# An attention-and-MLP kernel in new instruction orders, with fewer unused matmuls, and VectorE and GpSimd kept apart

## The chip, the cores and the metric

The kernel runs on one core of a Trainium2 chip. The core has five engines that run side by side, each in the order of its own instruction stream: TensorE (PE; its weight loads are listed apart as PEld), ScalarE (ACT), VectorE (DVE), GpSimd (POOL) and SyncE (SP, which here only issues DMA transfers). They wait for one another through semaphores. The metric is the device time of one execution in microseconds (us); smaller is better. Before the change it is 211.13 us, the median of three runs (210.77 to 211.39).

## The reference: decayed linear attention, then an MLP with a snake activation

Attention comes first, for 4 batches of 8 heads, 768 positions and 64 channels, in blocks, with a state that is carried from block to block. Its output, as 3072 tokens of 512 features, goes through an MLP of width 2048.

```python
for b in range(nb):
    intra = np.einsum('bhic,bhjc->bhij', qb, kb) * Dmask[None]
    intra = np.einsum('bhij,bhjd->bhid', intra, vb)
    inter = np.einsum('bhid,bhde->bhie', qb * lam_pow[None], kv_state)
    out[:, :, sl] = intra + inter
    kv_state = lam_block[None, :, None, None] * kv_state + np.einsum('bhsd,bhse->bhde', kb_dec, vb)
...
h = x @ w_in
s = np.sin(alpha * h)
g = h + s * s / (alpha + 1e-09)
return (g @ w_out).astype(np.float32)
```

## The kernel before

**Work.** Attention is done in 24 blocks of 128 positions (6 for each batch). A block's q and k are loaded as float32, scaled by powers of lam into bf16 (`scale_block`, L462 to L495, on DVE, POOL and ACT), transposed on PE or by DMA (`piece_Q`, `piece_K`, `piece_T`), multiplied into scores (`part_S`, L612) and masked on DVE (L623). Then come the state (`part_Z`, L648 and L656, evicted by L666 and L672) and the output (`part_O`, `piece_P` and `piece_I`, evicted by L726 and L739 into `xT`, the MLP's input, transposed). Four blocks are one chunk of 512 tokens; there are six chunks.

For each chunk and each of 16 slices of the MLP's width, `unit_A` (L822; `unit_A2`, L856, does two slices for half a chunk) multiplies w_in's slice with `xT`; ACT takes the sine (L832, L866); ACT or POOL squares it (L836 and L837, L870 and L871); DVE adds h (L839, L874) and writes `gT`. Chunks 0 and 1 are multiplied by w_out in `unit_B` (L887). For chunks 2 to 5 the second product is done with seven instead of eight block products (`product`, `unit_P`, L975). These need sums of blocks of `gT` and of w_out: `token_sums` (L953) and `weight_sums` (L930), each a TENSOR_TENSOR whose operands are all bf16 in SBUF, on DVE or POOL. `finish` and `finish_half` combine the products and store the result.

**Order.** `_Plan.op` doesn't issue anything: it appends an operation to a list of 1040, with its engine or the engines it may run on, and works out from the tiles read and written which earlier operations it depends on. `_Plan.ORDER` has a table for each engine (PE, ACT, DVE, POOL, SP) with the numbers of its operations in the order in which they are issued. Where an operation may run on two engines, the table in which its number stands decides. `_settle` takes the tables as they are, and `emit` issues the instructions with the waits that the dependencies ask for. An engine does its table strictly in order: an operation that waits holds up all behind it.

**Unused matmuls.** In PE's table a pair (n, cols) stands for n matmuls of `idle` (ones) with itself, 128 x 128 by `cols` columns, into bank 0, with a result that nobody reads (`spin`, L1134). `idle` is set by a DVE memset, op 16.

**Numbers that the prediction names.** Loads on SP: 2, 3 (q, first four blocks), 4 to 7 (k), 8 to 11 (v, in two pairs), 96 and 97 (w_in's first slices), 109 (q of blocks 4 and 5). Loads on POOL: 102 to 104 (w_in) and 105 to 108 (w_out). Start: 41 to 46, 49 and 50 scale q and k; 53, 55, 57, 59 transpose q, 61, 62, 69, 70 transpose k; 47 and 48 (POOL) cast v of blocks 0 and 1 from loads 8 and 9; 51 (ACT) and 52 (POOL) cast v of blocks 2 and 3 from loads 10 and 11; 29 and 30 (POOL) clear the two `Zd` tiles; 65, 67, 73, 78 are the scores of blocks 0 to 3; 75, 82, 87 the state after blocks 0 to 2, evicted on ACT by 76 and 77, 83 and 84, 88 and 89; 81, 86, 92, 94 evict the four outputs to `xT` (95, on DVE, half of the last); 124 and 130 are the first two units of chunk 0, which need blocks 0 and 1, and 2 and 3. Later: 195 and 196 (POOL) scale the two halves of q of blocks 4 and 5, 206 and 207 transpose them; 142, 149, 153 and others are squares; 232, 233, 235 are parts of `unit_B`; 653 is DVE's addition for a slice of chunk 3, 673 the PE piece that uses its bank, 681 a unit next to it. The end: 1028 is the product that the store 1030 needs, 1037 the last product.

Of the kernel before, what the change touches and what calls it, by code (L numbers as in the profile page):

```python
# [33 lines left out]
class _Plan:  # L34
# [17 lines left out]
        ),  # L52
        "ACT": (
# [16 lines left out]
        ),  # L70
        "DVE": (
# [1174 lines left out]
```

## Time and profile before

| | |
|---|---|
| median of three runs | 211.13 us (210.77 to 211.39) |
| profiled execution, span from its first to its last instruction | 209.8 us |
| instructions in it | 4867 |
| granted TensorE clock, as the profile shows it | 1.000 |
| HBM read, written | 27.28 MB, 6.29 MB |
| costliest group: L822 on PE, x296 | 70.5 us, 379 ns each |
| L975 on PE, its three largest groups | 16.3, 16.0 and 15.8 us |
| L887 on PE, x128 | 31.4 us, 380 ns each |

The profile is of one execution, taken by the hardware profiler. Busy time is the time in which at least one instruction of an engine ran. In a timeline row stand the start, the length, the engine, the line, the operation, the tiles out<-in, the shape and the count of instructions merged; a bracket gives the engine's idle time just before and what ended it. Ends of matmuls are modelled and overlap with the next start, so that starts tell the pace. In the chain of work that ended last a row has start, length and what it was. A row of a DMA queue has packets, megabytes and the share of 16 engines' time.

### The profile page before, as it was taken

To read this page: it belongs to the slowest core of one execution; us is meant where nothing else is said; L and a number is where in the kernel's file an instruction comes from. 1 tells how busy PE (TensorE), PEld (TensorE's weight loads), DVE (VectorE), ACT (ScalarE), POOL (GpSimd) and SP (SyncE) were. 2 spreads that over 40 slices of the span, in tenths; PEclk is the share of its full clock that TensorE was granted. 3 is DMA by queue.
4 is the path that set the end of the run, shared out by engine and by line. 5 is a ranking of instruction groups with operands and counts; after the bars stand their busy time and mean duration, and the time that the engine had idled before them with its cause. 6 is when DMAs were issued, how large, how long until landed. Compare 5 with 4: busy or idle time off the path is not lost.

```text
span 209.8 us, 4867 instructions
## 1 busy us (share of the span) xinstructions
PE 203.5 (97%) x1975; PEld 134.3 (64%) x1975; DVE 160.3 (76%) x266; ACT 158.7 (76%) x294; POOL 126.9 (60%) x130
## 2 busy tenths in 40 slices
PE   7979999999999999999998999999999999999995
PEld 6847444457677776555555667766667765666894
DVE  4884557563999866868899799889698699777643
ACT  4949995968998989999997887787963889568210
POOL 7075354994469578679885392944581957378300
DMA  4999999999998999999999920190000004000514
GB/s 141 310 318 232 206 213 237 246 229 256 220 264 205 227 245 230 223 233 196 246 271 228 213 53 0 33 271 2 3 0 3 0 23 179 3 0 0 200 40 163
DMA packets 78998, 33.35 MB, mean 159 GB/s; under 512 B 55408, under 2 KB 76160, under 8 KB 78976
## 3 DMA queue, kind: packets, MB, share of 16 engines
q1 hardware_dynamic: 73744, 27.14, 56.2%
q0 software_dynamic: 3696, 3.67, 10.5%
q10 hardware_dynamic: 1536, 2.24, 3.3%
q8 instruction: 15, 0.25, 0.5%
q14 instruction: 7, 0.06, 0.1%
HBM read 27.28 MB, written 6.29 MB: 160 GB/s over the span
## 4 chain that ended last, share of the span: by engine, by line
PE 83%; DVE 6%; DMA 3%; SPq 3%; ACT 2%; issue 1%
PE bank L822 27%; PE bank L975 22%; PE bank L887 13%; PE bank L856 10%; DMA v<-in_v_dram 3%; PE bank L716 3%; SPq L315 3%; PE bank L612 3%; DVE gT L839 2%; PE bank L694 1%; DVE Sm L623 1%; PE bank L511 1%; PE bank L656 1%; DVE w L930 1%; PE bank L534 1%; PE bank L707 1%
## 5 line engine op out<-in xcount | busy, mean ns | idle before, releaser
L822 PE MATMUL bank<-xT,w 128*128 128x512 bf16 x296 | 70.5, 379 | 0.0
L839 DVE SCALAR_TENSOR_TENSOR gT<-u,rinv,bank 128x512 bf16<-128x512 bf16 x74 | 53.6, 742 | 18.2 <-ACT u L836 12.5
L832 ACT ACTIVATE t<-bank,alpha 128x512 bf16<-128x512 f32 x74 | 50.0, 684 | 21.0 <-PE bank L822 20.5
L822 PEld LDWEIGHTS bank<-xT,w 128*128 128x128 bf16 x296 | 28.3, 98 | 28.4 <-DVE gT L839 0.4
L836 ACT ACTIVATE u<-t 128x512 bf16<-128x512 bf16 x59 | 36.5, 628 | 1.3
L837 POOL TENSOR_TENSOR u<-t 128x512 bf16<-128x512 bf16 x15 | 16.0, 1066 | 34.1 <-ACT t L832 30.5
L953 POOL TENSOR_TENSOR gT<-gT 128x512 bf16<-128x512 bf16 x24 | 27.8, 1172 | 11.2 <-DVE Xs L953 6.0
L623 DVE TENSOR_TENSOR Sm<-bank,mask 128x1024 bf16<-128x1024 f32 x24 | 29.1, 1218 | 4.3 <-PE bank L648 1.8
L887 PE MATMUL bank<-w,gT 128*128 128x512 bf16 x128 | 31.4, 380 | 0.0
L874 DVE SCALAR_TENSOR_TENSOR gT<-u,rinv,bank 128x256 bf16<-128x256 bf16 x44 | 18.8, 476 | 7.8 <-ACT u L870 6.1
L472 POOL TENSOR_TENSOR qk<-q,Lq 128x512 bf16<-128x512 f32 x20 | 21.2, 1075 | 2.8 <-DMA q<-in_q_dram 2.8
L856 PE MATMUL bank<-xT,w 128*128 128x256 bf16 x176 | 22.2, 273 | 0.0
L492 POOL TENSOR_TENSOR qk<-k,Lk 128x512 bf16<-128x512 f32 x20 | 20.9, 1053 | 0.6 <-DMA k<-in_k_dram 0.6
L866 ACT ACTIVATE t<-bank,alpha 128x256 bf16<-128x256 f32 x44 | 18.9, 476 | 2.0 <-PE bank L856 1.5
L887 PEld LDWEIGHTS bank<-w,gT 128*128 128x128 bf16 x128 | 11.7, 98 | 12.2
L856 PEld LDWEIGHTS bank<-xT,w 128*128 128x128 bf16 x176 | 16.4, 98 | 3.5 <-issue 0.3
L953 POOL TENSOR_TENSOR Xs<-gT 128x512 bf16<-128x512 bf16 x13 | 16.1, 1235 | 1.5 <-DVE gT L839 1.4
L975 PE MATMUL bank<-w,gT 128*128 128x256 bf16 (+1 forms) x136 | 16.3, 266 | 0.0
L975 PE MATMUL bank<-w,Xs 128*128 128x256 bf16 (+1 forms) x136 | 16.0, 267 | 0.1
L975 PE MATMUL bank<-ws,gT 128*128 128x256 bf16 x128 | 15.8, 273 | 0.0
L975 PEld LDWEIGHTS bank<-w,gT 128*128 128x128 bf16 x136 | 12.6, 98 | 3.2
L975 PEld LDWEIGHTS bank<-w,Xs 128*128 128x128 bf16 x136 | 12.4, 98 | 2.8 <-DVE osb L1021 0.3
(101 smaller groups left out, 276.0 us busy)
## 6 DMA issues: line engine op xcount, KB each, us to landing
q<-in_q_dram SPq DMA_DIRECT2D x12, 512.0 KB, 6.2
k<-in_k_dram SPq DMA_DIRECT2D x24, 256.0 KB, 5.5
v<-in_v_dram SPq DMA_DIRECT2D x24, 256.0 KB, 5.4
out_dram<-osb SPq DMA_DIRECT2D x14, 256.0 KB, 2.5
w<-in_moe_w_out_dram POOLq DMA_DIRECT2D x4, 512.0 KB, 11.4
w<-in_moe_w_in_dram POOLq DMA_DIRECT2D x3, 512.0 KB, 9.0
ws<-in_moe_w_in_dram SPq DMA_DIRECT2D x2, 512.0 KB, 7.5
out_dram<-osb ACTq DMA_DIRECT2D x8, 128.0 KB, 4.0
```

The costliest lines, as they stand in the source:

```text
L472: lambda e, a=a: e.tensor_tensor(qk2[:, j:j + 2, 4 * a:4 * a + 4, :], q32[:, jq, 4 * a:4 * a + 4, :, :].rearrange("p h t d -> p t h d"), b ...
L492: lambda e: e.tensor_tensor(qk2[:, j, H:2 * H, :], block32(k32, jl), lk, ALU.mult), 1.05,
L623: op("DVE", lambda e: e.tensor_tensor(Sm[js][:, :, :], banks[:, 512 * b0:512 * b0 + 1024].rearrange("p (c i) -> p c i", i=128), bass.AP(ma ...
L822: ins = e.matmul(ps[hb][:, c0:c1], w1[:, kc, 128 * m:128 * (m + 1)], xT[x][:, kc, c0:c1], start=(kc == 0 and c0 == lo), stop=(kc == NKC - ...
L832: op("ACT", lambda e: e.activation(t16[ju][:, w], ps[hb][:, w], ACTF.Sin, scale=alpha[:, m:m + 1]), 0.69 if hi - lo == TCH else 0.475, [ba ...
L836: lambda e: (e.activation(u16[ju][:, w], t16[ju][:, w], ACTF.Square) if e is nc.scalar else e.tensor_tensor(u16[ju][:, w], t16[ju][:, w], ...
L839: op("DVE", lambda e: e.scalar_tensor_tensor(out=gT[g][:, m, w], in0=u16[ju][:, w], scalar=rinv[:, m:m + 1], in1=ps[hb][:, w], op0=ALU.mul ...
L856: ins = e.matmul(ps[hb][:, 256 * i:256 * i + 256], w1[:, kc, 128 * (m + i):128 * (m + i + 1)], xT[x][:, kc, lo:lo + 256], start=(kc == 0 a ...
L866: op("ACT", lambda e, i=i: e.activation(t16[ju][:, 256 * i:256 * i + 256], ps[hb][:, 256 * i:256 * i + 256], ACTF.Sin, scale=alpha[:, m + ...
L887: ins = e.matmul(ps[ob][:, w], gT[g][:, m, 128 * s4:128 * (s4 + 1)], w2[:, m, w], start=(m == 0), stop=(m == NM - 1),)
L953: e.tensor_tensor(dst, in0, in1, alu), 0, rd, wr))
L975: ins = e.matmul(ps[ob][:, lo + d0:lo + d1], lhs, rhs[:, d0:d1], start=first and p == 0, stop=(p == NM // 2 - 1), skip_group_check=True)
```

## The change

The five tables of `ORDER` are replaced. The list of operations, the tiles, the dependencies and the functions are the same. What differs:

- the order of operations within each engine;
- the engine of 100 operations that may run on two: token sums between DVE and POOL (24 come to DVE, 21 leave it: 43 on DVE before, 46 after), weight sums (7 on DVE before, 5 after), squares between ACT and POOL, casts of v from ACT to POOL (5), and small evictions between ACT and DVE;
- the unused matmuls of PE: 102 in ten places before (42 of 112 columns, 51 of 128, 9 of 512), 30 of 512 columns in two places after: 24 at the start, 6 in front of op 67.

The first rows of each table and the end of PE's:

```diff
     ORDER = {
         "PE": (
-            (42,112), 39, (30,128), 57, (11,128), 55, (1,128), 53, (1,128), 59, (8,128), 61, (1,512), 62,
-            (3,512), 65, 67, 69, 70, (3,512), 73, 75, 78, 80, 82, 85, (2,512), 87, 90, 91, 93, 124, 130, 140,
-            136, 151, 155, 147, 144, 167, 163, 159, 230, 228, 175, 171, 229, 232, 231, 233, 183, 191, 187, 179,
-            235, 206, 207, 234, 209, 236, 217, 215, 237, 241, 221, 245, 319, 226, 320, 249, 250, 272, 252, 258,
+            (24, 512), 59, 55, 61, 39, 62, 53, 57, (6, 512), 67, 69, 70, 65, 78, 75, 73, 82, 80, 85, 87, 90, 91,
+            93, 124, 130, 140, 136, 147, 151, 155, 167, 163, 144, 159, 230, 175, 228, 171, 183, 229, 191, 179,
+            187, 231, 206, 207, 233, 232, 209, 234, 215, 217, 236, 235, 221, 237, 245, 226, 241, 272, 249, 250,
...
-            650, 655, 654, 661, 659, 681, 673, 720, 685, 691, 700, 680, 689, 716, 706, 705, 714, 735, 721, 730,
+            614, 650, 655, 629, 643, 648, 661, 681, 673, 680, 689, 691, 700, 685, 654, 706, 659, 716, 705, 714,
...
-            962, 972, 966, 976, 985, 977, 989, 990, 996, 994, 1006, 1004, 1010, 1002, 1008, 1012, 1023, 1015,
-            1021, 1025, 1034, 1028, 1018, 1031, 1037,
+            951, 947, 976, 961, 970, 962, 966, 985, 972, 977, 989, 990, 994, 996, 1002, 1004, 1010, 1008, 1006,
+            1015, 1012, 1018, 1025, 1021, 1031, 1023, 1028, 1034, 1037,
         ),
         "ACT": (
-            1, 31, 32, 34, 35, 36, 37, 38, 58, 40, 56, 54, 60, 63, 71, 72, 51, 76, 77, 81, 83, 84, 86, 88, 89,
-            92, 94, 125, 126, 127, 131, 132, 141, 133, 152, 137, 138, 148, 153, 145, 168, 164, 165, 156, 146,
+            1, 31, 32, 35, 34, 36, 37, 38, 60, 40, 56, 58, 54, 72, 71, 76, 77, 51, 84, 83, 81, 89, 88, 86, 92,
+            94, 126, 125, 127, 132, 131, 141, 133, 137, 138, 148, 152, 164, 168, 156, 160, 161, 176, 177, 172,
...
         "DVE": (
-            16, 17, 20, 19, 23, 33, 26, 28, 41, 42, 43, 44, 45, 46, 100, 49, 64, 101, 66, 68, 74, 79, 98, 95,
+            17, 16, 20, 33, 23, 19, 26, 41, 43, 44, 45, 46, 42, 49, 63, 100, 64, 68, 66, 79, 74, 98, 95, 28, 99,
...
         "POOL": (
-            12, 13, 14, 18, 15, 21, 22, 24, 25, 27, 29, 30, 50, 47, 48, 102, 103, 52, 105, 106, 104, 142, 107,
-            149, 169, 157, 108, 199, 195, 196, 197, 428, 431, 211, 212, 213, 219, 260, 255, 304, 261, 262, 280,
+            13, 18, 21, 22, 24, 25, 27, 12, 14, 15, 52, 50, 47, 29, 48, 30, 102, 103, 105, 199, 104, 142, 149,
+            153, 106, 169, 165, 157, 107, 108, 196, 195, 197, 181, 433, 211, 212, 213, 219, 260, 261, 304, 262,
...
         "SP": (
-            0, 2, 3, 4, 5, 6, 7, 8, 9, 10, 11, 96, 97, 112, 109, 110, 111, 113, 114, 116, 115, 117, 119, 118,
+            0, 2, 3, 4, 5, 6, 11, 7, 8, 9, 10, 96, 97, 112, 109, 110, 111, 113, 114, 120, 115, 117, 116, 119,
...
```

85 rows, old and new, of the table ORDER are left out of this document.

## The prediction

> **What bounds the kernel now.** I read the page's busy table and its chain, then the busy time of each engine stage by stage, then what each stage waits for.
>
> ```profile
> PE 203.5 (97%) x1975; PEld 134.3 (64%) x1975; DVE 160.3 (76%) x266; ACT 158.7 (76%) x294; POOL 126.9 (60%) x130
> ...
> PE 83%; DVE 6%; DMA 3%; SPq 3%; ACT 2%; issue 1%
> ```
>
> ```profile
> 0.00:19.00 19.00, 16.00 (x300) 12.82 (x301) 12.61 (x23) 13.02 (x28) 10.59 (x25) 1.00 0.99 255
> 19.00:104.00 85.00, 85.00 (x789) 51.04 (x788) 62.49 (x106) 74.59 (x147) 57.75 (x54) 1.00 1.11 229
> 104.00:124.00 20.00, 19.33 (x175) 12.03 (x172) 17.66 (x25) 17.34 (x31) 13.85 (x13) 1.00 1.02 210
> 124.00:198.00 74.00, 74.00 (x626) 50.16 (x624) 62.79 (x100) 53.00 (x89) 43.53 (x39) 1.00 0.15 49
> 198.00:210.00 12.00, 9.18 (x100) 8.25 (x98) 4.79 (x15) 0.75 (x2) 1.15 (x1) 1.00 0.30 103
> ```
>
> The columns after the stretch's length are PE, PEld, DVE, ACT and POOL busy, the granted clock, the DMA share and GB/s. From 19 us, where the first unit of the large product starts, to 198 us PE stands still for 0.67 us in all, all of it between 104 and 124. The change keeps every useful matmul. So nothing that it does for DVE, ACT or POOL between 19 and 198 can bring more than 0.67 us; the rest of any gain must come from the first 19 us or the last 12. A loss has no such lid: each moved matmul can meet an input that is not ready.
>
> **What the exclusion of VectorE and GpSimd costs now.** The first rows give the shortest, the median and the longest duration in ns, from the view of one source line; the others give busy time and mean, from the view of all groups.
>
> ```profile
> L953 DVE TENSOR_TENSOR gT<-gT x24: 409/418/1372, 98.2 to 200.2; 128x512 bf16<-128x512 bf16 x24
> L953 DVE TENSOR_TENSOR Xs<-gT x19: 407/419/1359, 92.1 to 196.2; 128x512 bf16<-128x512 bf16 x19
> ...
> L930 DVE TENSOR_TENSOR w<-w x3: 679/684/1951, 102.9 to 114.4; 128x1024 bf16<-128x1024 bf16 x3
> ```
>
> ```profile
> L953 DVE TENSOR_TENSOR Xs<-gT 128x512 bf16<-128x512 bf16 x19 | 12.3, 658 | 0.1
> L953 DVE TENSOR_TENSOR gT<-gT 128x512 bf16<-128x512 bf16 x24 | 12.2, 532 | 0.1
> ```
>
> The means (658, 532 ns) stand 0.24 and 0.12 us over the medians: 19 x 0.24 + 24 x 0.11 = 7.2 us, and 1.27 us for the one weight sum, 8.5 us in which DVE stood behind a POOL instruction. All but one of these lie beside busy PE. That one is:
>
> ```profile
> 108.17 2.30 POOL L930 TENSOR_TENSOR w<-w 128x1024 bf16<-128x1024 bf16 x1
> 109.07 1.95 DVE L930 TENSOR_TENSOR w<-w 128x1024 bf16<-128x1024 bf16 x1
> 112.32 0.40 PE L694 MATMUL bank<-qkT,Zd 128*128 128x128 bf16 x4 [0.56 <-DVE gT L839]
> ```
>
> DVE's sum ends at 111.02, just after POOL's (110.47); the L839 behind it is what PE waits for. An order that keeps the two apart takes 1.27 us from that chain: the 0.56 us go, if nothing else is then late. **Term 1: -0.55 us** (bounds 0 and -0.67).
>
> **Work changing engines.** By the diff 46 instead of 43 token sums and 5 instead of 7 weight sums run on DVE, ACT has 306 - 303 = 3 operations less and POOL 3 more. With all four stages above showing DVE, ACT and POOL below PE, this is worth nothing by itself; the cover is PE's own work, and what it costs without that cover is rival 2.
>
> **The start.** The first unit (op 124) needs q, k and v through scaling, transposes, masks and two evictions. Who waits there:
>
> ```profile
> 10.70 1.04 POOL L480 TENSOR_TENSOR qk<-k,Lp 128x512 bf16<-128x512 f32 x1 [5.41 <-DMA k<-in_k_dram]
> ...
> 13.61 0.62 POOL L486 CAST v<-v 128x512 bf16<-128x512 f32 x1 [1.31 <-DMA v<-in_v_dram]
> ```
>
> ```profile
> 14.49 0.62 ACT L486 CAST v<-v 128x512 bf16<-128x512 f32 x1 [1.18 <-DMA v<-in_v_dram]
> 15.01 0.75 ACT L666 CAST Zd<-bank 64x256 bf16<-64x256 f32 x2
> ...
> 18.85 1.04 ACT L739 CAST xT<-bank 128x512 bf16<-128x512 f32 x2
> ```
>
> ```profile
> 14.29 0.62 PE L648 MATMUL bank<-v,qk 64*128 64x128 bf16 x8 [0.90 <-POOL v L486]
> ...
> 18.99 2.07 PE L856 MATMUL bank<-xT,w 128*128 128x256 bf16 x16
> ```
>
> Loads land in the order of SP's queue: load 7 at 10.7, load 9 at 13.6, load 10 at 14.5, so 0.9 us for one place. The change puts load 11 ahead of 7, 8, 9 and 10, each one place later: load 9, whose cast (op 48) releases op 75 at 14.29, would come 0.9 us late. But two places took 2.9 us between 7 and 9, 1.1 us more than the pace. From 10.4 to 11.8 us an instruction fetch ran on the same DMA engines (the row of its queue in that stretch, and in the whole run):
>
> ```profile
> q8 instruction: 1, 0.02, 5.3%
> ```
>
> ```profile
> q8 instruction: 15, 0.25, 0.5%
> ```
>
> ```profile
> 0.00:10.50 10.50, 8.79 (x122) 8.07 (x122) 6.74 (x17) 7.45 (x16) 3.88 (x16) 1.00 0.83 225
> ```
>
> Fifteen such fetches for 2 x 1975 PE instructions are one for each 263: they are PE's, and the first comes when PE has started 122 + 122 = 244. Of those instructions 2 x 97 are unused matmuls and their loads. After the change PE has 2 x (30 unused + 81 useful) = 222 up to op 78 and 238 with op 75, so its first fetch comes with op 75 or later, behind the v loads. I take the pace without it: load 8 at 12.3, 9 at 13.2, 10 at 14.1. On POOL the cast 47 then ends at 13.1, the Zd memset (op 29), now between the two casts, at 13.6, and cast 48 at 14.1: op 75 starts at about 14.1 against 14.29. Behind it ACT is the chain: from 15.01 to 19.89 it hardly stops (three pairs of Zd at 0.75, four evictions in 2.5). The new ACT order puts cast 51, which now partly precedes that chain, inside it (0.53 us more), and op 86, which op 124 needs, behind 89 and 88. From op 75's end at 14.7: Zd 76 and 77 to 15.5, cast 51 to 16.1, Zd 84 and 83 to 17.0, evictions 81 to 17.7, Zd 89 and 88 to 18.45, 86 to 19.1, 92 and 94 to 20.2. So op 124 starts at 19.2 instead of 18.99 and op 130 at 20.25 instead of 20.03. **Term 2: +0.2 us** (bounds: -0.2, if casts and evictions pack as tightly as the best rows, +1.3, if the fetch still falls on the v loads).
>
> **The unused matmuls** (102 before, 30 after) lie in PE's waiting time; they cost nothing now and nothing when gone, unless the clock falls:
>
> ```profile
> 1.52 2.61 PE L1134 MATMUL bank<-Xs 128*128 128x112 bf16 x26 [1.52 <-DVE Xs L410]
> ```
>
> ```profile
> 5.16 1.85 PE L1134 MATMUL bank<-Xs 128*128 128x128 bf16 x30
> ```
>
> 26 matmuls of 112 columns start within 2.3 us (2.61 less the 0.3 that the last takes), 92 ns apart; 30 of 128 columns start 56 ns apart. So the clock doubles between 3.9 and 5.2, though the clock column says 1.00. The 24 new fills of 512 columns last at least as long (six at the slow rate, the rest at the fast one: to about 8.2), and the next useful op is ready at 8.3. Later I find no hole longer than today's 0.90 us before op 75. Term: 0.
> The Trainium skill ("TensorE: Matmul & The Clock Gate", section "What's actually happening") says that the clock goes back to half after about 3.4 us with too little activity. By that rule, with the fills between op 65 and op 87 gone, the units could start at half rate. That is rival 4; no row of before shows the clock falling.
>
> **Where matmuls are moved ahead.** The place with the least room is the first transposes of q for block 4 (ops 206 and 207):
>
> ```profile
> 36.24 2.04 POOL L472 TENSOR_TENSOR qk<-q,Lq 128x512 bf16<-128x512 f32 x2 [0.67 <-DMA q<-in_q_dram]
> ```
>
> ```profile
> 39.69 0.61 PE L534 MATMUL bank<-ident,qk 128*128 128x128 bf16 x8
> 40.13 1.03 PE L887 MATMUL bank<-w,gT 128*128 128x512 bf16 x4
> ```
>
> q lands at 36.2; op 195 follows at 37.28, op 196 at 38.28, PE comes at 39.69. In the new order three units of 0.87 us (232, 233, 235) stand behind op 206, so PE comes at 39.7 - 2.6 + 0.2 = 37.3; and POOL now does 196 before 195, so op 206 is released at q's landing plus 2.1 us, 38.3. That is 1.0 us of standing PE, unless q lands earlier. It may: w_out's second load (op 106) is issued later (behind 142, 149, 153 on POOL), and the queue of q has the DMA engines to itself for about a microsecond; I take half. **Term 3: +0.5 us** (0 to +1.0). What waits behind op 206 on PE is all of it.
>
> **The end.** The last product (op 1037) stays last with the same eviction and store. But the 256 KB store 1030 is now issued about a microsecond later, near the last ones:
>
> ```profile
> 205.45 0.42 DVE L1021 TENSOR_TENSOR osb<-kept,bank 128x256 f32<-128x256 f32 x1 [0.25 <-PE bank L975]
> ...
> 207.21 0.29 DVE L997 TENSOR_TENSOR osb<-kept,bank 128x128 f32<-128x128 f32 x1
> ```
>
> DVE's row at 205.45 moves behind the third-last product, to about 206.3. At the 103 GB/s of the last stretch the engines are mostly free. **Term 4: +0.1 us** (0 to +0.5).
>
> **Sum**: -0.55 + 0.2 + 0.5 + 0.1 = +0.25 us on the profiled span of 209.8, 210.05 us. The median of the runs, 211.13, lies 1.3 us over that span for what surrounds it; with the same margin the time is 211.4 us. Its own range from the bounds that I think likely is 210.8 to 211.8.
>
> **The rivals.**
> 1. *The v loads come a place late* (slower). If the first fetch still falls on loads 8 to 10, cast 48 ends at 15.2, op 75 starts 0.9 us late, and with ACT's order the first units start 1.3 us late: term 2 is +1.3, 212.5 us. For it: the order of the queue is certain. Against: the fetch count above. It decides from load 9 landing after 13.8. Chance 0.16.
> 2. *Matmuls moved ahead meet VectorE in the crowded stretch* (slower). From 104 to 124 DVE is busy 17.66 of 20 us. There the chain had:
>
> ```profile
> 120.90 0.74 DVE gT L839
> ```
>
> ```profile
> 122.13 0.39 PE L694 MATMUL bank<-qkT,Zd 128*128 128x128 bf16 x4
> ```
>
> The first row is op 653, which ends at 121.64 and releases op 673, the second row, 0.49 us before PE comes to it. In the new tables op 673 has two products (1.75 us) less ahead of it on PE, op 653 some 0.6 us more ahead of it on DVE: 1.75 + 0.6 - 0.5 = 1.85 us short, of which DVE regains 0 to 1.27 us at the weight sum. In the middle 1.2 us are lost: 212.6 us. It decides once DVE is over 0.5 us behind there. The same holds if the two engines collide as often as now, so that the order doesn't do what it says: then nothing is regained. Against: the orders are made for that very stretch. Chance 0.20.
> 3. *All fits* (faster): term 1 is -0.67, q lands early enough, the start gains 0.2, the end nothing: 211.13 - 0.9 = 210.2 us. Against: the bounds must all fall on one side. Chance 0.18.
> 4. *The clock falls before the first units.* The slow phase at the start lasts about 2.9 us in the rows (1.52 to some 4.4); one more of these over the units loses half, 1.45 us: 212.8 us. Against: no hole over 0.9 us. Chance 0.06.
>
> **How the numbers follow.** The forecast has 0.40. A measurement of this kernel tells about 0.3% (0.63 us) from no change, so faster means under 210.5 and slower over 211.76. Faster: 0.17 of rival 3 and 0.02 of the forecast, 0.19. Same: 0.36 of the forecast and 0.05 from the edges of the rivals, 0.41. Slower: the rest, 0.40. The range for 8 in 10 reaches from rival 3 to beyond rivals 1, 2 and 4: 210.2 to 213.3.
>
> **What would show it.** Right: PE busy without a gap of 0.5 us near 112; the first L856 at 19.2; the first fetch after 14 us and load 9's cast before 13.8; a wait of PE or its weight loads for POOL's L472 near 37 to 38; the first 30 us without matmuls at half rate. Wrong: first L856 after 20 (rival 1); waits of PE for DVE's L839 between 115 and 140 that sum to over 1 us (rival 2); L822 spaced over 400 ns apart (rival 4). The forecast as a whole is wrong if PE's gaps between 19 and 198 us sum to over 1.5 us.

## The result, and the profile after

The changed kernel takes 212.84 us, the median of five runs (212.15 to 213.39), against 211.13 (210.77 to 211.39 in five runs): a ratio of 1.0083, 95% interval 1.0064 to 1.0102. It is 1.7 us slower. A run more than 1.5% above the fastest of its kernel stays out of its ratio, which below concerns three of b_30's six runs alone. The profile is of the execution that took 213.39 us, with a span of 211.6; before's had 209.8. Lines of the code have moved up by two: L822 of before is L820 after, L856 is L854.

The busy table and the chain on the page of after:

```profile
PE 201.7 (95%) x1876; PEld 131.3 (62%) x1903; DVE 151.2 (71%) x266; ACT 155.7 (74%) x291; POOL 126.2 (60%) x133
...
PE 77%; DVE 10%; ACT 5%; DMA 3%; issue 3%; ACTq 1%; POOL 0%; DVEq 0%
```

VectorE's busy time fell from 160.3 to 151.2 us with the same 266 operations (the prediction counted 8.5 us spent behind GpSimd), while PE's share of the chain fell from 83 to 77%. PE has 1876 records for 1903 weight loads, so 27 records are missing, and each reads as up to 0.2 us of false idle time; starts are the safer measure. Why VectorE got faster stands in the views of lines L951 and L928 (shortest, median and longest duration in ns):

```profile
L951 DVE TENSOR_TENSOR gT<-gT x27: 409/418/425, 99.0 to 203.6; 128x512 bf16<-128x512 bf16 x27
...
L951 DVE TENSOR_TENSOR Xs<-gT x19: 411/420/678, 98.7 to 198.1; 128x512 bf16<-128x512 bf16 x19
```

```profile
L928 DVE TENSOR_TENSOR w<-w x3: 684/685/685, 111.3 to 119.9; 128x1024 bf16<-128x1024 bf16 x3
```

The longest were 1372, 1359 and 1951 ns before. The order does what it says: in these sums VectorE hardly ever stands behind GpSimd now. The stages, for the same stretches as before:

```profile
0.00:19.00 19.00, 16.42 (x221) 9.15 (x222) 12.24 (x22) 11.82 (x26) 9.26 (x24) 1.00 0.97 250
19.00:104.00 85.00, 81.63 (x760) 50.15 (x772) 59.38 (x104) 69.18 (x140) 57.25 (x57) 1.00 1.11 210
104.00:124.00 20.00, 19.67 (x169) 11.56 (x171) 17.23 (x31) 17.91 (x32) 11.63 (x9) 1.00 1.19 212
124.00:198.00 74.00, 73.05 (x610) 50.48 (x618) 56.59 (x94) 55.41 (x93) 44.74 (x43) 1.00 0.26 67
198.00:210.00 12.00, 10.95 (x124) 9.93 (x122) 5.76 (x18) 1.39 (x4) 3.37 (x3) 1.00 0.33 117
```

Most of PE's missing time lies in the second row, where it had none before: 3.37 us, part of it missing records; the four gaps over 0.25 us in it are 0.95, 0.77, 0.46 and 0.28 us long. PE's timeline of the first 21 us tells more (rows between left out):

```profile
1.66 7.96 PE L1132 MATMUL bank<-Xs 128*128 128x512 bf16 x24 [1.66 <-DVE Xs L408]
9.46 0.61 PE L532 MATMUL bank<-ident,qk 128*128 128x128 bf16 x8
...
14.32 0.42 PE L610 MATMUL bank<-qkT 64*64 64x128 bf16 x16 [0.43 <-DVE Sm L621]
14.67 0.62 PE L646 MATMUL bank<-v,qk 64*128 64x128 bf16 x8
...
18.71 0.34 PE L777 MATMUL bank<-qkT,Zd 128*128 128x128 bf16 x3
20.00 0.45 PE L777 MATMUL bank<-qkT,Zd 128*128 128x128 bf16 x5 [0.95 <-issue]
20.29 2.19 PE L854 MATMUL bank<-xT,w 128*128 128x256 bf16 x16
```

Op 124, the first L854, starts at 20.29 instead of 18.99, 1.30 us late. That is most of the 1.8 us by which the span grew. Just ahead of it op 91 (L777, four matmuls for each of ops 91 and 93) stops after its third matmul for 0.95 us. It waits for no semaphore: "issue". And it is the middle of one operation, whose inputs were all there. The row of the instruction queue in the stretch from 17.3 to 18.8 us:

```profile
q8 instruction: 1, 0.02, 5.2%
```

This is the first instruction fetch of the run (none lies ahead of 17.3); it ends at 18.68, 1.3 us before op 91 goes on. I read this as PE having run out of instructions; a_fill below tests it. Behind the start, the gap at 112 us is gone, and one wait is new, at op 234 (the row at 41.85) among PE's rows near 40 us and the weight loads' waits:

```profile
38.52 0.61 PE L532 MATMUL bank<-ident,qk 128*128 128x128 bf16 x8
38.97 1.89 PE L885 MATMUL bank<-w,gT 128*128 128x512 bf16 x8
...
41.85 0.81 PE L885 MATMUL bank<-w,gT 128*128 128x512 bf16 x3 [0.77 <-DVE gT L837]
```

```profile
PEld bank L885 <- DMA w<-in_moe_w_out_dram: 0.7, 1, 0.7
```

The matmul's row names VectorE, its weight load names w_out's load 107: the weights came last.

### The profile page after: what moved, and what is told of

It reads as the page before. It is cut to its first block, busy times and chain, and to the rows that moved or that the text cites. A ratio compares the mean times of both kernels' runs of the same rounds, so it can differ in the third digit from the quotient of the medians.

```text
span 211.6 us, 4711 instructions
## 1 busy us (share of the span) xinstructions
PE 201.7 (95%) x1876; PEld 131.3 (62%) x1903; DVE 151.2 (71%) x266; ACT 155.7 (74%) x291; POOL 126.2 (60%) x133
## 4 chain that ended last, share of the span: by engine, by line
PE 77%; DVE 10%; ACT 5%; DMA 3%; issue 3%; ACTq 1%; POOL 0%; DVEq 0%
PE bank L820 25%; PE bank L973 19%; PE bank L885 9%; PE bank L854 7%; PE bank L1132 4%; DVE gT L837 4%; PE bank L610 3%; DMA out_dram<-osb 3%; PE bank L714 3%; ACT t L830 2%; DVE gT L951 2%; PE bank L532 1%; PE bank L646 1%; ACT u L834 1%; DVE Sm L621 1%
## 5 line engine op out<-in xcount | busy, mean ns | idle before, releaser
L820 PE MATMUL bank<-xT,w 128*128 128x512 bf16 x281 | 68.4, 380 | 1.8 <-issue 0.5
L820 PEld LDWEIGHTS bank<-xT,w 128*128 128x128 bf16 x296 | 28.0, 98 | 29.4 <-DVE gT L872 0.9
L834 ACT ACTIVATE u<-t 128x512 bf16<-128x512 bf16 x59 | 36.7, 629 | 1.6 <-DVE gT L837 0.4
L951 POOL TENSOR_TENSOR gT<-gT 128x512 bf16<-128x512 bf16 x21 | 24.0, 1154 | 14.2 <-DVE gT L951 7.1
L885 PE MATMUL bank<-w,gT 128*128 128x512 bf16 x117 | 30.2, 380 | 1.7 <-DVE gT L837 0.8
L835 POOL TENSOR_TENSOR u<-t 128x512 bf16<-128x512 bf16 x15 | 15.4, 1036 | 25.0 <-ACT t L830 24.9
L854 PE MATMUL bank<-xT,w 128*128 128x256 bf16 x176 | 22.0, 273 | 0.1
L470 POOL TENSOR_TENSOR qk<-q,Lq 128x512 bf16<-128x512 f32 x20 | 20.5, 1042 | 0.0
L885 PEld LDWEIGHTS bank<-w,gT 128*128 128x128 bf16 x128 | 11.6, 98 | 12.6 <-DMA w<-in_moe_w_out_dram 0.7
L854 PEld LDWEIGHTS bank<-xT,w 128*128 128x128 bf16 x176 | 16.4, 98 | 3.9 <-DVE mask L422 0.4
L951 POOL TENSOR_TENSOR Xs<-gT 128x512 bf16<-128x512 bf16 x13 | 15.1, 1169 | 5.8 <-DVE gT L837 5.7
L973 PE MATMUL bank<-w,gT 128*128 128x256 bf16 (+1 forms) x136 | 15.5, 266 | 0.0
L973 PEld LDWEIGHTS bank<-w,Xs 128*128 128x128 bf16 x136 | 12.6, 98 | 3.3
L973 PEld LDWEIGHTS bank<-ws,gT 128*128 128x128 bf16 x128 | 12.5, 98 | 2.9 <-DVE gT L837 0.2
```

Source lines behind the costliest of these rows:

```text
L470: lambda e, a=a: e.tensor_tensor(qk2[:, j:j + 2, 4 * a:4 * a + 4, :], q32[:, jq, 4 * a:4 * a + 4, :, :].rearrange("p h t d -> p t h d"), b ...
L820: ins = e.matmul(ps[hb][:, c0:c1], w1[:, kc, 128 * m:128 * (m + 1)], xT[x][:, kc, c0:c1], start=(kc == 0 and c0 == lo), stop=(kc == NKC - ...
L834: lambda e: (e.activation(u16[ju][:, w], t16[ju][:, w], ACTF.Square) if e is nc.scalar else e.tensor_tensor(u16[ju][:, w], t16[ju][:, w], ...
L854: ins = e.matmul(ps[hb][:, 256 * i:256 * i + 256], w1[:, kc, 128 * (m + i):128 * (m + i + 1)], xT[x][:, kc, lo:lo + 256], start=(kc == 0 a ...
L885: ins = e.matmul(ps[ob][:, w], gT[g][:, m, 128 * s4:128 * (s4 + 1)], w2[:, m, w], start=(m == 0), stop=(m == NM - 1),)
L951: e.tensor_tensor(dst, in0, in1, alu), 0, rd, wr))
```

## The experiments

The twelve kernels differ from the two in orders and unused matmuls alone. "First fetch" and "op 124" are starts in us in the profile; the last column is the longest wait of PE behind op 124.

| kernel | ratio to before, 95% interval | first fetch | op 124 | longest wait of PE behind it |
|---|---|---|---|---|
| before | 1 | 10.50 | 18.99 | 0.56, op 624 |
| after | 1.0083, 1.0064 to 1.0102 | 17.42 | 20.29 | 0.77, op 234 |
| s_start | 1.0075, 1.0047 to 1.0104 | 17.31 | 20.25 | under 0.3 |
| s_rest | 1.0028, 1.0000 to 1.0057 | 10.66 | 19.14 | 1.41, op 221 |
| a_fill | 1.0050, 1.0026 to 1.0075 | 17.05 | 20.73 | under 0.3 |
| a_59 | 1.0064, 1.0040 to 1.0087 | 16.12 | 19.78 | 1.61, op 234 |
| a_96 | 1.0153, 1.0108 to 1.0197 | 12.21 | 23.08 | under 0.3 |
| b_recut | 0.9981, 0.9967 to 0.9996 | 14.84 | 18.27 | 0.29, op 624 |
| b_30 | 1.0445, 1.0382 to 1.0509 | 18.82 | 21.85 | 7.66, op 191 |
| s_act | 1.0008, 0.9996 to 1.0020 | 11.41 | 19.57 | under 0.3 |
| a_w2 | 1.0075, 1.0046 to 1.0103 | 16.78 | 20.31 | under 0.3 |
| rest_w2 | 1.0171, 1.0138 to 1.0204 | 11.36 | 18.94 | 2.35, op 183 |
| a_rep | 1.0116, 1.0091 to 1.0142 | 15.86 | 19.50 | 1.97, op 209 |
| hyb1 | 1.0133, 1.0094 to 1.0172 | 16.07 | 19.69 | 0.79, op 209 |

### Start or middle: s_start and s_rest

s_start has the change's tables up to op 101 and before's behind it; s_rest is the reverse. The seam in PE's table of s_start:

```diff
-            (42,112), 39, (30,128), 57, (11,128), 55, (1,128), 53, (1,128), 59, (8,128), 61, (1,512), 62,
-            (3,512), 65, 67, 69, 70, (3,512), 73, 75, 78, 80, 82, 85, (2,512), 87, 90, 91, 93, 124, 130, 140,
+            (24, 512), 59, 55, 61, 39, 62, 53, 57, (6, 512), 67, 69, 70, 65, 78, 75, 73, 82, 80, 85, 87, 90, 91,
+            93, 124, 130, 140,
```

> The change's orders and 30 unused matmuls up to op 101 and before's orders behind that. Theory (most of the loss is a late start, which PE carries to the end because it is never idle behind it): op 124 starts at 20.2 to 20.4 us, op 130 at 21.4, the 0.56 us gap near 112 us comes back, and the time is 212.3 to 212.6, some 1.2 us over before. Rival (the loss lies in the reordered middle): under 211.6.

> Before's orders and 102 unused matmuls up to op 101 and the change's orders behind that. Theory: op 124 starts at 19.0 as in before; the new waits behind it (w_out's second load 0.9 us, three waits of 0.2 to 0.45 us for DVE and ACT) less the waits that went (0.56 us at 112, 0.27 at 123) leave +0.3 to +0.7, 211.4 to 211.8. Rival (the loss lies in the reordered middle): 212.4 or more. Third case (the middle alone is a gain): under 210.9.

Measured: s_start 212.53 against 211.10 us, s_rest 211.88. The start alone carries nearly the whole loss, the middle alone about 0.6 us with an interval that just reaches nothing. Op 124 came at 20.25 as told, but by another way. Rows of s_start's stages and of its PE:

```profile
12.00:16.40 4.40, 3.54 (x97) 2.51 (x100) 3.79 (x4) 2.49 (x7) 4.40 (x8) 1.00 1.13 325
16.40:19.80 3.40, 3.40 (x78) 2.67 (x72) 1.43 (x2) 2.38 (x6) 2.47 (x3) 0.50 1.26 216
```

```profile
18.71 1.07 PE L754 MATMUL bank<-Sm,v 64*64 64x128 bf16 x32
...
20.25 2.17 PE L851 MATMUL bank<-xT,w 128*128 128x256 bf16 x16
```

The granted clock is 0.50 for 3.4 us, and 32 matmuls of L754 take 1.07 us where the same op took 0.64 after the change. The slow PE needs its instructions later (its 222nd matmul starts at 19.84, the fetch ended at 18.61), so there is no gap. One start, two ways to lose about the same: dry of instructions at full clock, or half clock. The granted clocks of the runs tell how often: a stretch of 3.4 us at half would show as 0.992, and the change's five runs have 0.998 to 1.000, while five of s_start's twelve have 0.984 to 0.992 (212.21 to 213.99 us). The other seven, at 1.000, take 212.17 to 212.96, so the loss is there without the clock.

The 0.56 us gap near 112 us, which term 1 counted on, did not come back in s_start as I had expected, though it has before's orders there; PE's row for 104 to 125 us:

```profile
104.00:125.00 21.00, 20.89 (x187) 13.14 (x186) 17.59 (x27) 18.85 (x33) 14.81 (x13) 1.00 1.00 212
```

In s_rest the wait of op 221 is ScalarE's, for a cast of v whose load came late:

```profile
ACT v L492 <- DMA v<-in_v_dram: 3.0, 1, 3.0
```

Its twelve runs fall apart: 210.85 to 211.67 in six, 212.10 to 212.86 in six; the profile (212.56) is of the upper ones. In this stretch loads of SP and of GpSimd's queue share the DMA engines, and with w_out's loads 107 and 108 issued at 31.69 and 32.49 us v's load, issued at 25.5, landed at 43.7. I take the sharing for the cause; no run separates it.

### The fetch: a_fill, a_59, a_96

The change with its first 24 unused matmuls re-cut, nothing else:

```diff
-            (24, 512), 59, 55, 61, 39, 62, 53, 57, (6, 512), 67, 69, 70, 65, 78, 75, 73, 82, 80, 85, 87, 90, 91,
+            (44, 280), 59, 55, 61, 39, 62, 53, 57, (6, 512), 67, 69, 70, 65, 78, 75, 73, 82, 80, 85, 87, 90, 91,
```

with (59,208) for a_59 and (96,112) for a_96.

> The change with 44 unused matmuls of 280 columns in place of 24 of 512: the same work of PE (12,320 against 12,288 columns), 40 more instructions. Theory (PE runs dry of instructions in op 91, because its first fetch is asked for too late): the fetch comes some 2 us earlier (15 to 16.5 us), still behind the v loads; op 91 runs through without its gap of 1.1 us, op 124 starts 0.6 to 0.7 us earlier, near 19.6, op 130 near 20.7, and the time is 212.0 to 212.3. Rival (the gap in op 91 or the late start come from the clock's later rise, the order of ACT or the loads): the gap stays, op 124 at 20.2 or later, 212.7 to 213.

> The change with 59 unused matmuls of 208 columns in place of 24 of 512 (12,272 columns of work), so that PE starts its 150th instruction, behind which the first fetch came 3.2 to 4.6 us later in six profiles, near 10.8 us instead of 12.8 to 13.2. Theory (PE runs dry because the fetch is late): fetch at 14.2 to 15.3 us, just behind the v loads; no gap in ops 90 and 91; op 124 at 19.5 to 19.8 and op 130 at 20.7, 0.65 us earlier than after the change; 211.7 to 212.2. Rival (the late start is ACT's order and the clock alone): op 124 at 20.2 or later, 212.5 or more. If the granted clock falls to half between 14 and 20 us in the profile, the run says nothing of the fetch.

> The change with 96 unused matmuls of 112 columns in place of 24 of 512: 10,752 columns, and before's count of instructions. Theory (the fetch follows the count of instructions that PE has started): the first fetch lies at 10.8 to 12.3 us, among the v loads, and makes those behind it about 1.1 us late; op 75 starts at 15.2 or later instead of 14.67, op 91 has no gap, op 124 starts at 20.2 to 20.8: 212.6 to 213.2. Rival (loads and fetch do not meet): op 75 at 14.7, op 124 near 19.6, 212.1.

a_fill missed: the fetch came only 0.4 us earlier, and the gap did not go, it moved, with op 124 at 20.73. That the time, 212.22, lies in the range told all the same is luck. PE's rows:

```profile
18.36 0.41 PE L755 MATMUL bank<-Sm,v 64*64 64x128 bf16 x15
19.88 0.46 PE L755 MATMUL bank<-Sm,v 64*64 64x128 bf16 x17 [1.11 <-issue]
```

It stands after 15 of op 90's 32 matmuls instead of after op 91's third: 17 + 3 = 20 matmuls earlier, as many as were added. So the gap belongs to a fixed number of PE instructions (222 matmuls had run in both), not to an operation, as the end of a page of instructions would and a late input would not. And it ends with the fetch: in all seven profiles that have such a gap (after, a_fill, a_59, b_recut, b_30, a_rep, hyb1), it stands after 221 or 222 matmuls, and PE goes on 1.3 to 1.6 us after the first fetch ended, wherever that was between 15.97 and 19.76 us. Why the fetch itself moved by only 0.4 us the rows don't settle; in both kernels PE comes to its first scores at 12.6 or 12.8 us, and I take the instruction that starts the fetch to lie near there.

a_59 gets the fetch 1.3 us earlier than after the change, at 16.12, still 0.8 us later than told. PE waits 0.34 us after 65 unused and 157 other matmuls, 222 again, and op 124 starts at 19.78, in the range told:

```profile
18.65 0.64 PE L755 MATMUL bank<-Sm,v 64*64 64x128 bf16 x32 [0.34 <-DVE w L380]
...
19.78 2.09 PE L852 MATMUL bank<-xT,w 128*128 128x256 bf16 x16
```

The profile puts the 0.34 us down to VectorE's cast of w, which op 90 does not read; by the count it is the fetch. The time (212.57) missed; in the profile 1.61 us at op 234 ate the gain. a_96 puts the fetch at 12.21, on the v loads: load 9 lands at 15.37, 2.0 us later than in a_fill, where I had told 1.1, op 75 waits 1.48 us, to 16.32, and then the clock falls to half:

```profile
16.32 0.62 PE L644 MATMUL bank<-v,qk 64*128 64x128 bf16 x8 [1.48 <-POOL v L482]
...
23.08 2.60 PE L852 MATMUL bank<-xT,w 128*128 128x256 bf16 x16
```

```profile
17.60:24.40 6.80, 6.61 (x99) 5.29 (x100) 2.64 (x5) 4.60 (x10) 3.66 (x5) 0.50 1.00 165
```

The direction was right, the size not (214.63 instead of at most 213.2): op 75 is 1.65 us later than after the change, and from there to op 124 it takes 6.76 us at half clock, against 4.94 in b_recut below.

### The fetch in the kernel before: b_recut and b_30

b_recut cuts before's unused matmuls into fewer pieces of the same sum of columns; b_30 gives it the change's 30.

```diff
-            (42,112), 39, (30,128), 57, (11,128), 55, (1,128), 53, (1,128), 59, (8,128), 61, (1,512), 62,
+            (22, 214), 39, (14, 274), 57, (7, 201), 55, (1, 128), 53, (1, 128), 59, (5, 205), 61, (1, 512), 62,
```

> The kernel before with its unused matmuls cut otherwise: (42,112) as (22,214), (30,128) as (14,274), (11,128) as (7,201), (8,128) as (5,205), the same columns of work in 43 fewer matmuls; all orders as before. Theory (a fetch on the DMA engines delays the loads behind it by 1.1 us, and its time follows the count of PE's instructions): the first fetch comes at 12.8 to 14.0 us instead of 10.5, behind load 9; load 9 lands at 12.3 to 13.3 instead of 14.46, op 75 starts 0.7 to 1.1 us earlier than 14.29, op 124 at 18.2 to 18.6 instead of 18.99: 210.3 to 210.7, faster than before. Rival (the fetch's place is of no weight): op 75 at 14.3, 211.1.

> The kernel before with one part of the change alone: its 102 unused matmuls replaced by the change's 30 (24 of 512 columns first, 6 ahead of op 65). Theory (fewer unused matmuls move PE's first fetch behind the v loads, where it is too late for PE): fetch at 15.8 to 17.4 us instead of 10.5 to 11.4; loads 9 to 11 land 1.1 us earlier than before (load 9 at 13.2 or earlier); PE stands 0.4 to 1.2 us without a releaser at its 222nd matmul, op 91, or the clock falls to half there; op 124 at 19.4 to 20.2, so the earlier loads are given back: 211.1 to 211.9. Rival of the prediction (the unused matmuls cost nothing and gain nothing, the earlier loads remain): no such gap, op 124 at 18.1 to 18.7, 210.4 to 210.8.

b_recut is the only kernel faster than before: 210.67 against 211.21 us in twelve and seventeen runs. PE's rows:

```profile
13.33 0.62 PE L644 MATMUL bank<-v,qk 64*128 64x128 bf16 x8
...
18.27 2.19 PE L852 MATMUL bank<-xT,w 128*128 128x256 bf16 x16
```

The fetch comes at 14.84, later than told, behind the v loads: load 9 lands at 12.38 instead of 13.56 (the 14.46 that I gave for it is load 10's) and the last at 14.17. Op 75 starts at 13.33 instead of 14.29 and op 124 at 18.27 instead of 18.99. PE waits 0.19 us for its instructions, no more. This is the place for the fetch: late enough for the loads, early enough for PE. The start gains 0.72 us, the time 0.5.

b_30 shows the other side, far beyond what either theory told: 224.33 us. Its load 9 lands 1.2 us earlier than before's, but PE comes to op 75 only at 15.19, 0.9 us late, for the long unused matmuls hold its first transpose to 9.44 (7.20 in before). The gap is where it was expected, and the clock falls within it. PE's row behind it, the longest wait of PE, and two stages:

```profile
21.26 0.80 PE L774 MATMUL bank<-qkT,Zd 128*128 128x128 bf16 x6 [1.73 <-issue]
```

```profile
PE bank L817 <- DVE gT L834: 7.7, 1, 7.7
```

```profile
20.20:27.00 6.80, 5.74 (x27) 3.56 (x27) 1.90 (x4) 3.35 (x7) 0.00 (x0) 0.50 1.25 208
...
44.10:54.30 10.20, 5.00 (x12) 1.79 (x13) 7.92 (x5) 1.33 (x3) 6.43 (x6) 0.50 1.06 202
```

With the gap and the half clock VectorE's weight sum (op 430) comes at 38.10, 5 us later than before, and meets GpSimd. VectorE's row, and GpSimd's:

```profile
38.10 10.49 DVE L925 TENSOR_TENSOR Ta<-w 128x1024 bf16<-128x1024 bf16 x1
```

```profile
36.85 1.06 POOL L487 TENSOR_TENSOR qk<-k,Lk 128x512 bf16<-128x512 f32 x1
37.86 2.04 POOL L467 TENSOR_TENSOR qk<-q,Lq 128x512 bf16<-128x512 f32 x2
39.86 1.03 POOL L487 TENSOR_TENSOR qk<-k,Lk 128x512 bf16<-128x512 f32 x1
40.86 4.18 POOL L925 TENSOR_TENSOR ws<-w 128x1024 bf16<-128x1024 bf16 x2
45.00 2.03 POOL L467 TENSOR_TENSOR qk<-q,Lq 128x512 bf16<-128x512 f32 x2
47.00 2.49 POOL L487 TENSOR_TENSOR qk<-k,Lk 128x512 bf16<-128x512 f32 x2
```

A sum of 0.68 us takes 10.49: it comes while GpSimd runs instructions back to back, and ends where that row is first stretched (2.49 us for two that take 2.1). Op 191 on PE waits 7.7 us for the L834 behind it, and PE's clock falls once more. In the profile of before this sum and the next of VectorE (op 429) stood just ahead of that chain of GpSimd:

```profile
32.86 0.68 DVE L930 TENSOR_TENSOR Ta<-w 128x1024 bf16<-128x1024 bf16 x1
...
35.40 0.73 DVE L930 TENSOR_TENSOR ws<-w 128x1024 bf16<-128x1024 bf16 x1
```

The second ended at 36.13, 0.1 us before GpSimd began (its row at 36.24 stands in the prediction). The six runs of b_30 scatter from 218.62 to 227.07, and the profile (226.88) is of one of the longest. Their granted clocks, 0.961 to 0.983, put the half clock at some 7 us in the shortest run and 17 in the longest (an estimate: twice the missing share of the span). How much of the loss is the gap, the clock or VectorE's long sum is not separated.

### ScalarE's order: s_act

```diff
-71, 72, 51, 76, 77, 81, 83, 84, 86, 88, 89, 92, 94
+72, 71, 76, 77, 51, 84, 83, 81, 89, 88, 86, 92, 94
```

> The kernel before with one part of the change alone: ScalarE's order from op 71 to op 94 as after the change (72, 71, 76, 77, 51, 84, 83, 81, 89, 88, 86, 92, 94 in place of 71, 72, 51, 76, 77, 81, 83, 84, 86, 88, 89, 92, 94). Theory (ScalarE is the chain behind op 75, and casts and zero states put ahead of the evictions make the first units late, term 2 of the prediction): op 124 at 19.3 to 19.8 us instead of 18.99, 211.5 to 212.0. Rival (ScalarE has room there, and all of the late start comes from the unused matmuls and the fetch): op 124 at 18.9 to 19.1, 211.0 to 211.3.

211.16 against 210.90 us, 1.0008 with an interval across 1: the rival by its time. In the profile op 124 did come late, by the wait that the theory names:

```profile
19.57 2.01 PE L852 MATMUL bank<-xT,w 128*128 128x256 bf16 x16 [0.23 <-ACT xT L735]
```

Against the profile of before that is 0.58 us late, 0.26 of it already at op 75 (14.55), since the unused matmuls ran slow for longer in that execution (op 59 at 9.58 against 8.63). The end does not show it: before's execution had the 0.56 us gap at 112, this one has none. By the ratio ScalarE's order costs 0.17 us, 0.42 at the interval's end.

### The middle: a_w2, rest_w2, a_rep, hyb1

Four attempts to have the change's orders behind op 101 with their loads in time. The edit of GpSimd's table in a_w2 and rest_w2:

```diff
-105, 199, 104, 142, 149, 153, 106, 169, 165, 157, 107, 108
+105, 106, 104, 199, 142, 107, 149, 153, 169, 165, 157, 108
```

a_rep has 105, 104, 106, 142, 107, 199, 149 and so on, and (59,120) for (24,512); hyb1 has b_recut's start with 102, 103, 52, 105, 104, 106, 142, 107, 149, 153, 169, 165, 157, 108, 199, 195, 196, and 233, 232 ahead of 206, 207.

> The change with the w_out loads 106 and 107 issued earlier, as before (GpSimd's order 105, 106, 104, 199, 142, 107, 149, 153, 169, 165, 157, 108). Theory (op 234's wait of 0.92 us is w_out's load, late because its issue stands behind 142, 149 and 153): no wait at op 234; q's load for op 206 lands later than 31.6 us (36 in before), and PE waits there for 0 to 1.0 us, by term 3 of the prediction; in all 212.1 to 212.9. Rival (the wait only moves: the loads share the same DMA engines): 212.8, with a new wait of about 0.9 us between op 206 and op 245.

> Before's start, the change's orders behind it, and the w_out loads as in before. Theory (behind the start the new order gains once its loads are in time): the 1.4 us wait of op 221 for v's load, which came with the later w_out loads, goes; the runs lie near the lowest of the same kernel without this edit, 210.6 to 211.2, at or below before. Rival (the waits in 36 to 46 us only move): 211.6 to 212.3.

> The change with 59 unused matmuls of 120 columns in place of 24 of 512 (7,080 columns, so they end 1 to 2 us earlier) and w_out's loads 106 and 107 ahead of GpSimd's 142 and 199. Theory (what the change lost lies in three places: the length of the unused matmuls, the late fetch, the late w_out loads): op 59 at 8.3 to 8.7 instead of 9.46, fetch at 14.2 to 15.3, no gap at ops 90 and 91, op 124 at 19.1 to 19.5, no wait at op 234: 211.0 to 211.7. Rival (the reordered work behind the start is itself slower): 212 or more with the start as told.

> Before's start with the unused matmuls cut in 43 fewer pieces, the change's orders behind op 101, the w_out loads issued as in before but 104 ahead of 106, op 199 behind 108, op 195 ahead of 196, and units 233 and 232 ahead of the transposes 206 and 207. Theory (the start gains 0.5 us by the fetch's place and the middle 0.3 to 0.6 us by DVE and GpSimd kept apart): op 124 at 18.2 to 18.6, no wait over 0.3 us behind it, 209.9 to 210.4, faster than before and than the re-cut alone (210.67 against 211.21). Rival (loads and order behind op 101 hang together, and each change of one brings a new wait): 211 or more.

a_w2 took op 234's wait away and brought none at op 206, though q's load landed at 35.45 instead of 31.59. The time stayed at 212.59; in its profile the start ran at half clock (0.53 from 16.4 to 19.8 us), as in s_start. The other three, at 214.57, 213.32 and 213.68 us, missed what their theories told; rest_w2 is slower than after the change, a_rep and hyb1 lie above it with intervals that overlap. rest_w2's waits:

```profile
PE bank L819 <- DMA w<-in_moe_w_in_dram: 2.4, 1, 2.4
...
PE bank L819 <- DVE w L381: 0.9, 1, 0.9
```

With 106 ahead of 104, w_in's load 104 lands at 35.13, and the change's PE order reaches op 183 at 32.9, 2.35 us too early. And VectorE's cast L381, for op 140, takes 2.19 us (0.69 in before) while GpSimd issues load 104 and runs op 199. a_rep's op 59 came at 8.35 as told, its fetch only at 15.86, with a gap of 0.61 us. There k's load landed at 40.79, while w_out's three landed at 33.64, 37.17 and 40.80; PE waited 1.97 us for GpSimd's scaling of that k, and the clock fell:

```profile
42.80:46.20 3.40, 3.40 (x19) 1.34 (x17) 2.30 (x3) 1.76 (x4) 3.40 (x4) 0.50 1.27 265
```

hyb1 lost 0.80 us to the fetch (at 16.07, since its unused matmuls ran slow for longer than in b_recut: op 59 started at 9.66 against 8.50) and 0.79 at op 209, behind transposes that my edit had put back to back. So the times bear out hyb1's rival, that loads and order behind op 101 hang together; with several pieces moved at once in a_rep and hyb1, no run shows which of them costs what.

## Why the prediction came out as it did

The time lies in the range of 210.2 to 213.3 and over 211.76, from where the prediction calls it slower (chance 0.40, against 0.41 for no clear change). But the sum, +0.25 us on the span, was not what happened: the span grew by 1.8. That the range held is luck: it reached so far for rivals 1, 2 and 4, and none of these was the cause. By its own last sign the forecast as a whole is wrong, for PE's four gaps named above, all between 19 and 198 us, sum to 2.5 us, over 1.5.

**What bounds the kernel: right.** VectorE lost 9.1 us of busy time and nothing came of it; PE bounds.

**Term 1 (-0.55): right in kind, too large.** The gap at 112 is gone. But s_start, with before's orders there, has none either: it comes and goes with the execution (0.56 us in before, 0.29 in b_recut, none over 0.25 in s_act). The profiled execution of before was itself long for its kernel: another run of before with a span of 209.4 took 211.14 us, so the margin around the span is 1.74, and the span of a median run 0.4 under the one that I summed on.

**Term 2 (+0.2): the step that failed, by size.** Its first half held: the fetch did move behind the v loads, and these landed evenly, 0.9 us apart. But op 124 came at 20.29 where I had 19.2, +1.30 over before. Of the 1.09 us that I missed, 0.57 are there at op 75 (14.67 instead of 14.1), where two things end together. PE's new order puts op 78 ahead of op 75, and op 78 waits for VectorE's mask to 14.32, because the scores before it came late behind the long fills; and cast 48 ended at 14.61 instead of 14.1, since the loads landed 0.4 us later in this execution than I had taken. In a_59 cast 48 ended at 14.21 and op 75 still came at 14.75, so the first is enough by itself. The other 0.52 come between op 75 and op 124, for which I had 5.1 us. a_59 takes 5.03 and s_act 5.02, and in both op 124 starts right behind op 86, the eviction on ScalarE that it needs (ended at 19.73 and 19.52): this is ScalarE's chain in its new order, and near my sum. After the change op 86 ended at 19.63, and op 124 came 0.66 us later, 5.62 behind op 75. That is the fetch. A fetch that comes later for the loads comes later for PE too, and this I left out. Before, it ended at 11.69, and PE came to the place at 15.3; after, it ended at 18.68, 0.4 us before PE had done its 222 matmuls, and PE went on 1.3 us after it. Cast 48 and op 86 after the change:

```profile
14.00 0.61 POOL L484 CAST v<-v 128x512 bf16<-128x512 f32 x1
```

```profile
18.91 0.72 ACT L737 CAST xT<-bank 128x512 bf16<-128x512 f32 x1
```

The Trainium skill ("Runtime: NRT & Kernel Launch", section "Instruction fetch mechanics") says that the sequencer fetches the next 16 KiB, 256 instructions, while the current page runs, so that crossing a page is mostly hidden. The fetches of this case have that size and pace (before, 15 with 0.25 MB together, one for each 263 instructions); here one of them was not hidden, for 0.95 us after the change and 1.73 us in b_30.

**Unused matmuls (term 0): wrong.** I said they cost nothing when gone unless the clock falls. The 24 fills ran to 9.46 us instead of 8.2 (9.04 and 9.17 in s_start and a_w2), and their count moves the first fetch, though not by the rule that I used: 244 instructions of PE had started when it came in before, 262 in a_96 and 356 after the change. In the kernel before, re-cutting the unused matmuls gains 0.2%, and exchanging them for the change's costs 4.45%.

**Term 3 (+0.5): the size by luck, for another load.** No wait at op 206; q landed at 31.59 instead of 36.17, so the "unless" of that step held in full. Its price was paid where I did not look: the same later issue on GpSimd made w_out's load 107 late for op 234 (0.77 us). s_rest prices the middle and the end at +0.6 us (0 to 1.2), where the sum had -0.55 + 0.5 + 0.1 = +0.05.

**Term 4 (+0.1):** the span grew by 1.8 us, of which 1.77 are there when the last product starts (208.34 against 206.57); nothing is left for the end.

**Rival 1** gave the number (+1.3 us at the first units, 212.5) by luck, with the wrong mechanism: load 9 landed at 13.63 us, before its 13.8. **Rival 2** did not come: from 120.59, eight matmuls of 0.216 us lead to 122.32, and op 673 starts at 122.55, so VectorE costs 0.2 us there:

```profile
120.59 2.13 PE L820 MATMUL bank<-xT,w 128*128 128x512 bf16 x7
122.55 0.39 PE L692 MATMUL bank<-qkT,Zd 128*128 128x128 bf16 x4
```

**Rival 4** (chance 0.06) was in none of the change's five runs, but it was in the profiles of s_start and a_w2, which have the same start up to op 101: too small a chance. Its "no hole over 0.9 us" was no protection; s_start has none over 0.43 between 9 us and the fall at 16.4. The Trainium skill ("TensorE: Matmul & The Clock Gate", section "What's actually happening") says that the clock is set by activity in a free-running window of about 3.4 us. The rows agree: half clock came in stretches of 3.4, 6.8 and 10.2 us, and with the same start in two profiles and not in a third.

**Open:** why the clock falls in some executions of this start and not in others, what asks for the first fetch, and what a start and a middle fitted to each other would bring; a_w2 and hyb1 did not reach it.

## What to carry to other kernels

Count the instructions of the bounding engine when you add, drop or re-cut idle ones: the count moves its instruction fetches, and a fetch among critical loads delays these, while one behind them may leave the engine dry; look for "issue" waits in the middle of an operation. An order of instructions leans on arrival times: a part of it moved by a microsecond or two meets other loads and other waits between VectorE and GpSimd, so price each moved piece with the lateness of what precedes it, and test start and rest apart. A wait of PE of some 1.5 us or more may cost twice, once by itself and once by the clock: it did in a_96 (1.48) and a_rep (1.97), and did not in a_59 (1.61) and rest_w2 (2.35).

## What the hardware showed unexpectedly

- PE stood still in the middle of an operation for want of instructions: 0.95 us after the change, 1.11 in a_fill, 1.73 in b_30; always when 221 or 222 matmuls had run.
- The clock fell to half for 3.4 us though no gap of PE just before was longer than 0.43 us (s_start), and for 10.2 us at one of 7.7 (b_30). The same 24 fills at the start ended at 9.04 us in s_start, at 9.46 after the change.
- One VectorE instruction with all operands in SBUF, 0.68 us long, took 10.49 us behind back-to-back GpSimd instructions: it did not get in after the first of them (b_30).
- Beside two loads of 512 KB on GpSimd's queue, a load of SP's queue came some 6 us late: in s_rest v's load landed 6.8 us after the k load ahead of it, where it was 0.7 after the change (33.43 against 32.73), with those two issued at 32.97 and 33.77.
